# Two linear-attention and MLP layers on one core: half of layer one's sum of phi(K) moved from TensorE to GpSimd and VectorE, with a new written-out order

## The chip, the core and the metric

The kernel runs on one core of a Trainium2 chip. The core has five engines that run side by side and wait for one another by semaphores: TensorE (PE in the profile; its weight loads are PEld), VectorE (DVE), ScalarE (ACT), GpSimd (POOL) and SyncE (SP), which here only issues DMAs. Matmul results land in PSUM, eight banks of 128 x 512 fp32; everything else works in SBUF. The metric is the device time of one execution in microseconds (us), the median of the runs shown. Lower is better.

## What is computed

The reference takes x (2048 tokens of 512 features, bf16) through four residual steps: attention block, MLP block, and both again with the same weights.

```python
# attention block, on y = layernorm(x), 32 heads of 16
q, k, v = split(y @ wqkv)
phi = lambda t: where(t > 0, t + 1, exp(t)) + 1e-6
kv  = einsum("bhsd,bhse->bhde", phi(k), v)
z   = einsum("bhsd->bhd", phi(k))               # sum of phi(k) over all tokens
o   = einsum("bhqd,bhde->bhqe", phi(q), kv) / (einsum("bhqd,bhd->bhq", phi(q), z) + 1e-6)
x   = x + o @ wo
# MLP block
x   = x + gelu(layernorm(layernorm(x)) @ w1 + b1) @ w2 + b2
```

The change is about z in the first of the two layers: for each of the 512 features of K, the sum of phi(K) over 2048 tokens.

## The kernel before

**Tiles.** Tokens are cut into 16 tiles of 128 (numbered 0 to 15) and these into four chunks of four. A tile of x has 128 tokens on the partitions and 512 features in the free dimension. Chunk c of x is one slot of the buffer t4.

**Layer one, start.** For each tile: statistics on DVE (`statsA0_n`, L775, and `aggrA0_n`, L777; tile 3's on ACT), the variance plus epsilon (`veps`, L782, on POOL or DVE), its power -0.5 on POOL (`pow`, L784), sometimes the negated mean times that (`nmr`, L795, POOL), and the norm on DVE (L803) or ACT (L798). Tiles 0 to 3 are transposed by PE (L825) and copied out by ACT (L835), tiles 0 and 1 from a version that is only centred (L789). For Q, and for all other tiles, the transpose is a DMA that SP issues (`TA0_n`, L812). Then come `K0_n` (L879, four matmuls of 128x512), phi of it, and `G0_n` (L984), which adds y^T phi(K) up in four PSUM banks that stay taken through the first 45 us; so K and Q share the other four. Q of chunk 0 is L909 and has features on the partitions; Q of the other chunks is L896 and has tokens on the partitions.

**phi** (function `phi`) is exp on ACT (L847), relu on ACT (L858), min with 1 on DVE (L851 or L860, called `mink` or `minq`), and a sum on DVE or POOL (L864). For tiles marked "max" there is no relu: DVE reads the bank once more (L853). A bank is free for the next K or Q when the last of these that read it is done.

**The sum z** (function `attn_z`). For each chunk c of layer one, `Z0_c` is 16 matmuls (L970): a 128x128 block of phi(K) as the weights, one column of ones as the moving operand, four tiles added up for each of four feature blocks. `zs0_c` on DVE copies (c = 0, L944) or adds (L941) the 128x4 result into `zs`. In layer two it is done another way for chunks 0 to 2: `za1` to `za11` add the phi(K) tiles up in the fp32 tile `zacc` (L958, on POOL or DVE), `zhi` (L923) rounds the sum to bf16 in `dz`, `zlo` (L926) takes the rest in bf16, and `ZH` (L933, L934) runs eight one-column matmuls, two for each feature block, on the two halves.

**What needs z.** `zb0` on DVE (L1040) spreads zs over a mask; `D0_0_k` on PE (L1100) takes zb as its weights and gives the denominators of chunk 0, whose logarithm and exponential ACT takes (L1102, L1104). `dz0` on DVE (L1045) and `ZR0` on PE (L1048) give zs as a row, which ACT copies (`cpz0`, L997) and the other chunks' denominators use (`pz`, L1077; `pr`, L1089 or L1108).

**After that**: G is copied to gtb (L1000, `cpg`), multiplied with Wv (L1034), masked (L1053, `kvm`), multiplied with Wo (L1057), and for each tile come the attention's output (L1123), its residual add, the norms of the MLP, the MLP's first matmul (L1153) with gelu on ACT (L1158), and the second (L1190). The last tile's is split (L1176).

**The order** is written out: `CONF` holds one list of operation names for each engine (`ORDER`), the buffer slot of each tile (`PLACES`) and the engine that does an operation where there is a choice (`WAY`). `Settled` takes these as they stand, `assign_waits` sets the semaphore waits, and each engine runs its list from front to back. Every operation waits for its inputs and for the readers of whatever lay in its slot before. `LOADS` names the first DMAs in their order. The `za` adds are one chain, since each reads and writes zacc.

The lines of `attn_z` that choose between the two ways, in before and after alike:

```python
by_sum = [int(v) for v in (eng("zc0") or "").split()] if L == 0 else list(range(NC - 1))
...
if L == 0 and by_sum and c == max(v for v in range(NC) if v not in by_sum):
    fold(True)
```

`eng("zc0")` looks the name up in `WAY`. Without it `by_sum` is empty in layer one.

Of the kernel before, what the change touches and what calls it, by code (L numbers as in the profile page):

```python
# [185 lines left out]
def assign_waits(graph, order, sems, dma_sems):  # L186
# [10 lines left out]
    while len(done) < total:  # L197
        moved = False
        for e in ENGINES:
# [84 lines left out]
        "act":  # L284
# [1075 lines left out]
```

## Time and profile before

| what | us |
|---|---|
| median of 3 runs | 323.21 (323.02 to 324.14) |
| the profiled execution | 323.1 |
| its span, first to last instruction | 321.9 |
| PE busy | 318.0 |
| DVE / ACT / POOL busy | 218.1 / 189.3 / 145.5 |

How to read it: the span is the time from the first to the last instruction of the profiled execution, and the execution's own time has a little around it. Busy times are sums over the span; matmuls are pipelined, so a PE that is busy may still be held up between matmuls, and the chain of work that ended last tells where. The granted TensorE clock was 1.00 throughout. The prediction quotes whole lines of the page and of answers of the trace. A line of a group gives line of code, engine, operation, output<-inputs, count, and times. A timeline line gives start and length in us. Line numbers are those of the kernel before; in the kernel after they are one higher from `build_kernel` on.

### The profile page before, as it was taken

Reading aid. Unit: us, or ns where it says so; the run is one execution under the profiler, and the core shown is the slowest. Engines: PE = TensorE matmul, PEld = TensorE weight load, DVE = VectorE, ACT = ScalarE, POOL = GpSimd, SP = SyncE. Lnnn points to the kernel's source line nnn. Section 1 sums busy time; section 2 is a strip of 40 time slices with the busy share of each in tenths; the row PEclk is TensorE's granted clock in tenths of the full one; section 3 lists DMA queues with packets and bytes.
Section 4 is the critical chain, followed back from the end, with each engine's and each line's share of the span. In section 5 each row is a group of like instructions: output and inputs, shape, how many; then the busy total and the mean of one; then the engine's idle time right before and its main releaser. Section 6 shows DMA issues by size and latency. Waiting matters only on the chain.

```text
span 321.9 us, 4748 instructions
## 1 busy us (share of the span) xinstructions
PE 318.0 (99%) x1703; PEld 157.4 (49%) x1703; DVE 218.1 (68%) x529; ACT 189.3 (59%) x324; POOL 145.5 (45%) x216
## 2 busy tenths in 40 slices
PE   8999999999999999999999999999999999999997
PEld 3444554666444444444444444558544444444444
DVE  5998789999786774028848899999889881101103
ACT  5898656797730636667962367979634442663320
POOL 6573978688655355101822415887454163000000
DMA  7844793142121412111010200122232322201002
GB/s 257 200 81 85 241 348 85 35 82 36 33 49 34 82 33 51 34 33 32 18 40 10 51 16 0 35 51 52 50 62 54 98 65 67 49 0 35 16 33 65
DMA packets 52355, 21.68 MB, mean 67 GB/s; under 512 B 47532, under 2 KB 50860, under 8 KB 52332
## 3 DMA queue, kind: packets, MB, share of 16 engines
q1 hardware_dynamic: 50844, 16.37, 22.4%
q0 software_dynamic: 1056, 4.72, 4.3%
q10 hardware_dynamic: 432, 0.30, 0.3%
q8 instruction: 13, 0.21, 0.3%
q14 instruction: 10, 0.08, 0.1%
HBM read 8.00 MB, written 2.10 MB: 31 GB/s over the span
## 4 chain that ended last, share of the span: by engine, by line
PE 97%; DMA 2%; DVE 0%; issue 0%
PE ps L1153 30%; PE ps L1190 29%; PE ps L1123 9%; PE ps L879 8%; PE ps L896 6%; PE ps L984 4%; PE ps L1013 4%; DMA t<-in_A_x_dram 2%; PE ps L909 2%; PE ps L1176 1%; PE ps L970 1%; PE ps L1034 1%; PE ps L1057 1%; PE ps L1100 1%; DVE stats L775 0%; PE ps L1048 0%
## 5 line engine op out<-in xcount | busy, mean ns | idle before, releaser
L1158 ACT ACTIVATE gT<-ps,b1c 128x512 bf16<-128x512 f32 (+1 forms) x140 | 77.0, 601 | 68.7 <-PE ps L1153 68.1
L1153 PE MATMUL ps<-t,w 128*128 128x512 bf16 (+1 forms) x560 | 102.5, 336 | 0.0
L1190 PE MATMUL ps<-w,gT 128*128 128x512 bf16 x434 | 98.6, 379 | 0.0
L1153 PEld LDWEIGHTS ps<-t,w 128*128 128x128 bf16 x560 | 54.8, 98 | 43.7 <-ACT gT L1158 0.2
L1190 PEld LDWEIGHTS ps<-w,gT 128*128 128x128 bf16 x434 | 42.5, 98 | 50.4
L784 POOL TENSOR_TENSOR rstd<-veps,neghalf 128x1 f32<-128x1 f32 x64 | 39.0, 625 | 41.1 <-DVE veps L782 38.9
L847 ACT ACTIVATE eb<-ps 128x512 bf16<-128x512 f32 x62 | 35.4, 606 | 19.3 <-PE ps L896 7.3
L1200 DVE TENSOR_TENSOR yb<-ps,xsb 128x512 bf16<-128x512 f32 x15 | 10.2, 688 | 41.4 <-PE ps L1190 41.4
L775 DVE BATCH_NORM_STATS2 stats<-xsb 128x6 f32<-128x512 f32 x48 | 32.0, 681 | 0.3
L1123 PE MATMUL ps<-gtb,t 128*128 128x512 bf16 x128 | 31.4, 379 | 0.0
L879 PE MATMUL ps<-wqkv,t 128*128 128x512 bf16 x128 | 30.9, 379 | 0.3 <-ACT t L835 0.3
L858 ACT ACTIVATE rb<-ps 128x512 bf16<-128x512 f32 x43 | 25.3, 607 | 5.8 <-PE ps L879 5.8
L798 ACT ACTIVATE yb<-xsb,nmr,rstd 128x512 bf16<-128x512 f32 x21 | 16.9, 814 | 15.1 <-POOL nmr L795 15.1
L896 PE MATMUL ps<-wqkv,t 128*128 128x512 bf16 x96 | 24.1, 379 | 0.0
L1089 POOL TENSOR_TENSOR t<-t,rr 128x512 bf16<-128x512 bf16 x18 | 19.3, 1072 | 9.0 <-DVE rr L1085 6.4
L782 POOL TENSOR_SCALAR veps<-mv 128x1 f32<-128x1 f32 x35 | 8.2, 236 | 32.7 <-DVE mv L777 31.3
L1196 DVE TENSOR_TENSOR xsb<-ps,xsb 128x512 f32<-128x512 f32 x16 | 10.8, 678 | 17.9 <-PE ps L1190 17.9
L1139 POOL TENSOR_TENSOR xsb<-xsb,b2b 128x512 f32<-128x512 f32 x17 | 21.4, 1267 | 3.0 <-DVE yb L803 2.9
L1077 POOL TENSOR_TENSOR lr<-t,zrow 128x512 f32<-128x512 bf16 x14 | 16.5, 1179 | 7.3 <-ACT zrow L997 4.5
L1123 PEld LDWEIGHTS ps<-gtb,t 128*128 128x128 bf16 x128 | 12.5, 98 | 14.5
L803 DVE TENSOR_SCALAR yb<-xsb,mv,rstd 128x512 bf16<-128x512 f32 x27 | 14.5, 542 | 7.3 <-POOL rstd L784 6.0
L879 PEld LDWEIGHTS ps<-wqkv,t 128*128 128x128 bf16 x128 | 12.1, 98 | 14.7 <-ACT t L835 0.9
(99 smaller groups left out, 363.7 us busy)
## 6 DMA issues: line engine op xcount, KB each, us to landing
w<-in_B_w_dram POOLq DMA_DIRECT2D x4, 896.0 KB, 9.1
out_dram<-yb SPq DMA_DIRECT2D x15, 128.0 KB, 2.0
t<-in_A_x_dram SPq DMA_DIRECT2D x3, 512.0 KB, 4.8
t<-yb SPq DMA_TRANSPOSE x62, 2.5
wqkv<-in_A_wqkv_dram SPq DMA_DIRECT2D x1, 512.0 KB, 5.9
wqkv<-in_A_wqkv_dram POOLq DMA_DIRECT2D x1, 512.0 KB, 4.7
wo<-in_A_wo_dram POOLq DMA_DIRECT2D x1, 512.0 KB, 5.3
t<-in_A_x_dram SPq DMA_DIRECT2D x1, 384.0 KB, 3.3
```

The lines of the kernel that those rows point to most:

```text
L775: G.op("dve", lambda e: e.bn_stats(stats[:, s.slot, :], src()), 620, reads=src_keys, writes=[k + "s"], tiles=[s, *src_tiles], name=f"stats ...
L784: G.op("pool", lambda e: e.tensor_tensor(rstd[:, s.slot:s.slot + 1], veps[:, s.slot:s.slot + 1], neghalf[:], op=ALU.pow), 570, reads=[k + ...
L847: G.op("act", lambda e: e.activation(eb[:, et.slot, :], bank(bt), ACT.Exp, scale=by()), 478, reads=[src_key, *more_keys], writes=[f"e{tag} ...
L858: G.op("act", lambda e: e.activation(rb[:, rt.slot, :], bank(bt), ACT.Relu, scale=by()), 478, reads=[src_key, *more_keys], writes=[f"r{tag ...
L879: ins = e.matmul(bank(b), lhsT=yTa(yT)[:, dt, k * P:(k + 1) * P], rhs=wqkv[:, dt, D:2 * D], start=(i == 0 and n == 0), stop=(i == len(part ...
L896: ins = e.matmul(bank(b), lhsT=yTa(yT)[:, dt, k * P:(k + 1) * P], rhs=wqkv[:, dt, 0:D], start=(dt == 0), stop=(dt == DT - 1))
L1089: lambda e, d=d, tok=tok, heads=heads: e.tensor_tensor(heads(tok()), heads(tok()), rr[:, d.slot, :].unsqueeze(2).broadcast_to([P, H, DH]), ...
L1123: ins = e.matmul(bank(wb), lhsT=yTa(pq)[:, kt, k * P:(k + 1) * P], rhs=gtb[:, kt, :], start=(kt == 0), stop=(kt == DT - 1))
L1139: G.op("pool" if on_pool else "dve", lambda e: e.tensor_tensor(xsb[:, st, :], xsb[:, st, :], b2b[:], op=ALU.add), 1120 if on_pool else 600 ...
L1153: ins = e.matmul(bank(b, n), lhsT=w1[:, dt, ft * P:(ft + 1) * P], rhs=yTa(yT)[:, dt, k0 * P:k1 * P], start=(dt == 0), stop=(dt == DT - 1))
L1158: G.op("act", lambda e, ft=ft, b=b, k0=k0, k1=k1, n=n: e.activation(gT[:, g.slot, ft * 512 + k0 * P:ft * 512 + k1 * P], bank(b, n), ACT.Ge ...
L1190: ins = e.matmul(bank(b), lhsT=gT[:, g.slot, ft * 512 + k * P:ft * 512 + (k + 1) * P], rhs=w2[:, ft, :], start=(ft == 0), stop=(ft == FT - 1))
```

## The change

Only `CONF` changes; no line of the functions does. One entry is added, and it takes chunks 0 and 1 of layer one through the way that layer two has:

```diff
-        "za9": "pool",
+        "za8": "pool", "za9": "dve", "zaA2": "dve", "zc0": "0 1",
```

So `Z0_0`, `Z0_1`, `zs0_0` and `zs0_1` are gone. In their place stand `zaA1` to `zaA7`, which add the phi(K) of tiles 0 to 7 up in zacc (`zaA2` on DVE, the other six on POOL), `zhiA`, `zloA` on DVE, `ZHA` on PE with eight one-column matmuls, and `zshA` on DVE, which adds its result to zs. `Z0_2` and `Z0_3` stay.

`ORDER`, `PLACES` and `WAY` are written anew for the whole kernel. `LOADS` and the place of the x loads among SP's operations are as before: the third chunk's load, `xc2`, still stands behind `TA0_0` and `TA0_1`. 36 operations go from POOL to DVE and 24 from DVE to POOL (`pz`, `pr`, `b2`, `veps`, `za`), the rest stay on their engines. The lists around the change, cut to where the sums are made and used:

```diff
 "pe":
-  PTA0_3 K0_2 K0_3 G0_0_0 G0_1_0 Q0_0_2 Q0_0_1 Q0_0_0 K0_5 G0_2_0 K0_4 Z0_0 G0_3_0 Q0_1_0 K0_7 Q0_1_3 K0_6
-  G0_4_0 G0_5_0 Q0_1_2 K0_13 K0_14 G0_6_0 K0_12 Z0_1 K0_15 K0_10 K0_8 K0_9 K0_11 G0_7_0 Q0_1_1 Z0_3 Q0_0_3
-  Z0_2 G0_8_0 G0_9_0 D0_0_2 G0_10_0 D0_0_0 G0_11_0 ZR0
+  PTA0_3 K0_2 K0_3 G0_0_0 G0_1_0 Q0_0_0 Q0_0_1 Q0_0_2 Q0_1_0 K0_4 G0_2_0 G0_3_0 K0_5 K0_7 K0_6 G0_4_0 Q0_1_3
+  G0_5_0 K0_15 Q0_1_2 K0_12 K0_13 G0_6_0 K0_14 K0_10 K0_8 K0_11 K0_9 G0_7_0 Q0_0_3 Z0_3 G0_8_0 Z0_2 Q0_1_1
+  ZHA G0_9_0 D0_0_2 G0_10_0 ZR0 G0_11_0
 "dve":
-  normA0_0 vepsA0_1 normA0_2 statsA0_5 normA0_3 aggrA0_5 normA0_1 statsA0_4
+  normA0_2 normA0_0 normA0_1 statsA0_4 normA0_3
...
+  phik0_3 minq0_0_1 zaA2 aggrA0_12 mink0_4 statsA0_10 vepsA0_12 phik0_4 phiq0_0_1 aggrA0_10 statsA0_11
+  statsA0_8 aggrA0_11 normA0_12 mink0_5 aggrA0_8 phik0_5 minq0_1_0 minq0_0_0 phiq0_1_0
...
-  phik0_9 phik0_11 zs0_2 zs0_3 zb0
+  mink0_8 zhiA phik0_10 mink0_9 mink0_11 phik0_9 phik0_11 zloA zs0_2 minq0_0_3 zs0_3 zshA zb0 dz0
 "pool":
+  powA0_4 vepsA0_7 powA0_7 vepsA0_5 nmrA0_7 zaA1 powA0_5 vepsA0_6 vepsA0_13 powA0_13 powA0_6 nmrA0_13 vepsA0_15
+  powA0_15 vepsA0_14 nmrA0_15 powA0_14 nmrA0_14 zaA3 powA0_12 zaA4 vepsA0_10 powA0_10 nmrA0_10 vepsA0_11
+  vepsA0_8 zaA5 powA0_8 nmrA0_8 powA0_11 nmrA0_11 vepsA0_9 powA0_9 zaA6 zaA7 phik0_14 phik0_8 b1z wv wo
 "sp":
-  xc1 wq xc3 TA0_0 TA0_1 xc2 TA0_5 TA0_4 TA0_7 TA0_6 TA0_13 TA0_14
+  xc1 wq xc3 TA0_0 TA0_1 xc2 TA0_4 TA0_7 TA0_5 TA0_6 TA0_13 TA0_15
```

The other orders differ all through in the same manner, by neighbours that change places.

469 rows, old and new, of tables (ORDER, PLACES, WAY) are left out of this document.

## The prediction

> **What bounds the kernel now.** I read the busy shares of the page first, then the waits of PE, then the chain that ended last. All times are us of the profiled execution: span 321.9, its own time 323.1, so 1.2 lie around the span; the median of the runs shown is 323.21, 0.11 above it.
>
> The page's busy times, by engine:
>
> ```profile
> PE 318.0 (99%) x1703; PEld 157.4 (49%) x1703; DVE 218.1 (68%) x529; ACT 189.3 (59%) x324; POOL 145.5 (45%) x216
> ```
>
> PE is busy 99% of the span, the others far less. The page warns that a busy PE need not be at its peak, so the next view is who PE waited for, over the whole span:
>
> ```profile
> PE ps L749 <- PEq L1345: 0.8, 1, 0.8
> PE ps L825 <- DVE yb L803: 0.5, 1, 0.5
> PE ps L879 <- ACT t L835: 0.3, 1, 0.3
> PE ps L825 <- DVE yb L789: 0.2, 1, 0.2
> ```
>
> 1.8 us in four waits. The chain that ended last (start, length, what) tells where they end:
>
> ```profile
> 8.09 0.69 DVE stats L775
> 8.79 0.33 DVE yb L803
> 9.12 0.04 issue
> 9.16 0.40 PE ps L825 x4
> 9.56 1.73 PE ps L879 x8
> ...
> 18.19 0.38 PE ps L970 x16
> 18.57 0.89 PE ps L984 x4
> ```
>
> Until 9.16 the start waits for the load of x's second chunk (lands 8.07), the statistics queued behind it on DVE, and the fourth tile's norm. From 9.16 the chain is PE alone to 319.94, every 128x512 matmul 0.216 after the last (0.86 for four). So from 9.16 on the time is the sum of what PE is given, and a removed matmul shortens it by its spacing, provided no new wait appears. L970 is the sum of phi(K) that the change halves: 16 one-column matmuls take 0.38, and the group behind them 0.89 instead of 0.86, so 0.41 a call.
>
> **What it removes and adds on PE.** Removed: Z0_0 and Z0_1, 2 x 0.41 = 0.82. Added: ZHA, 8 matmuls of one column. Its like is layer two's ZH (L933/L934): first matmul 189.24, next group 189.44, so 0.20. Net on PE: 0.62 less. Everything else on PE is the same set in another order (1703 - 32 + 8 = 1679 matmuls).
>
> **The wait it adds.** The sums zs feed zb, zb feeds D0_0_2 (L1100). In before, these rows stand there (timeline):
>
> ```profile
> 37.08 0.36 DVE L941 TENSOR_TENSOR zs<-ps,zs 128x4 f32<-128x4 f32 x2 [0.77 <-PE ps L970]
> 37.48 0.69 DVE L1040 TENSOR_TENSOR zb<-bdmask,zs 128x512 bf16<-128x512 bf16 x1
> ...
> 38.63 0.38 PE L1100 MATMUL ps<-t,zb 128*128 128x512 bf16 x1
> ```
>
> zb ends at 38.17, D0_0_2 starts at 38.63: two groups G (2 x 0.86) cover it, with 0.46 to spare. In the new order only G0_9 stands between ZHA and D0_0_2. From ZHA's start: 0.34 to the end of its last matmul, 0.04 to DVE, 0.15 for zs, 0.04, 0.69 for zb, 0.06 to PE (as from yb at 9.10 to L825 at 9.16) = 1.32. PE has 0.20 + 0.86 = 1.06 to do. So 0.26 of idle PE is new. Behind D0_0_2 everything on PE waits too. If the chain is shorter than these rows it is nothing; a DVE instruction ahead of zs could add one length, 0.69, but DVE then stands before zs waiting for it.
>
> **The adds.** Layer two has the same instruction; the rows of the tile zacc give POOL 1156/1158/1337 ns (min/median/max) and DVE 658/688/694. Six on POOL are 6 x 1.16 = 7.0 us, one on DVE 0.69, then the two halves 0.42 and 0.68 (rows L923, L926) and zs 0.15, less two zs of 0.15: DVE +1.6. In the stretch from 12.1 to 29.2, where the adds must run, POOL is busy 10.3 of 17.1 us: with 7.0 more it is full, to about 29.3. What is queued behind them are the powers and means of later x tiles (L784, L795), which DVE's and ACT's norms wait for, then SP's transposes, then PE. I laid the new order out from 9.16 with the durations of these rows, PE in steps of 0.86:
> - zaA1 must wait for phi(K) of tile 1 (about 11.8), and runs to 13.3. The power of tile 5 is behind it (13.9 instead of 10.3), its norm on DVE about 14.8, its transpose goes out behind tile 7's at 14.9 and takes the 2.5 of the DMA rows: 17.4. K0_5 is the 12th group after 9.39, at 18.9: 1.5 to spare.
> - The first transposed tile now is tile 4's (norm 12.1, issued 12.15, landed about 14.7), needed at 15.4 by Q0_1_0: 0.7 to spare, where before tile 5 landed at 15.1 for a use at 15.4.
> - Later transposes go out 1.31 apart from 17.5, two or three us before their K.
> - zaA7 ends at 29.2; phik0_14 behind it has its inputs at about 30.4. The halves end near 35.4, ZHA is reached near 37.0. All hidden.
> - wv's load, issued by POOL behind phik0_8, leaves some 1 us later (33.5 instead of 32.5), lands at 38, and KV uses it at 45.
>
> So the adds cost nothing as long as DVE keeps these dates. DVE is 27.4 of 30.8 us busy from 9.16 to 40; 1.6 more makes 94%, so that cover is thin.
>
> **Start, loads, tail.** The list of loads is unchanged; the load of x's third chunk still stands behind TA0_0 and TA0_1 on SP. The norm of tile 1 moves ahead of the statistics that wait for chunk two, so TA0_1 leaves at about 8.8 instead of 9.52 and that load about 0.7 sooner: nobody waits for it. The norm of tile 3 still stands behind statistics of chunk two (now tile 4's), so 9.16 stays. The last PE groups and the output are in the same order. These count zero. pr0_0_0 moves from POOL to DVE ahead of the copies of G (L1000): the last copy that KV needs ends some 0.2 to 0.3 before its use; zero too.
>
> **Sum.** -0.82 + 0.20 + 0.26 = -0.36: 323.1 - 0.36 = 322.7 by the profiled execution, 322.85 by the median. I say **322.8**.
>
> **The rule against it.** When a DVE instruction meets a long POOL one, rows show it stretched (timeline at 153 and at 156):
>
> ```profile
> 153.05 1.68 POOL L1139 TENSOR_TENSOR xsb<-xsb,b2b 128x512 f32<-128x512 f32 x1
> 153.06 0.66 DVE L958 TENSOR_TENSOR zacc<-zacc,pkb 128x512 f32<-128x512 f32 x1
> ...
> 153.63 1.25 DVE L860 TENSOR_SCALAR eb<-eb 128x512 bf16<-128x512 bf16 x1
> ```
>
> ```profile
> 156.32 1.22 POOL L864 TENSOR_TENSOR pkb<-eb,rb 128x512 bf16<-128x512 bf16 x1 [0.24 <-DVE eb L860]
> 156.44 0.68 DVE L853 SCALAR_TENSOR_TENSOR pkb<-ps,eb 128x512 bf16<-128x512 f32 x1
> ...
> 157.05 0.78 DVE L864 TENSOR_TENSOR pkb<-eb,rb 128x512 bf16<-128x512 bf16 x1
> ```
>
> L860 takes 0.285 at the median and 1.25 here, ending when POOL ends; L864 on DVE 0.42 elsewhere, 0.78 here. Statistics (L775, 0.63 to 0.70 everywhere) and the form reading PSUM (L853) are not touched. The Trainium skill, "SBUF — State Buffer", section "Who interferes with whom", says why: GpSimd and VectorE share a pair of ports under an exclusive lock, taken by whichever starts first for its whole instruction, and a VectorE instruction with two SBUF inputs or in a two-port mode blocks against it. The trace agrees with 1.25 for 0.285. By the rows that I laid out the sum is 322.8; by that rule, with the adds ahead wherever an add and such a VectorE instruction come free together, it is the second rival's 323.8.
>
> **Rivals.**
> 1. The wait at D0_0_2 is hidden after all (ZHA arrives late behind another short wait, or zb is quicker): the full 0.62, 322.5. For it: 0.26 is a sum of small parts. Against: each part is a row. Chance 0.12.
> 2. **Slower: an add takes the ports ahead of a DVE instruction that frees a PSUM bank.** Two places meet: zaA3 and mink0_4, both free to start near 18.2 (both follow zaA2); zaA5 and minq0_0_0, both near 22.9 (both follow phik0_5). Price 1.25 - 0.285 = 0.96 each. Behind the first stands phik0_4 (ends near 20.0), whose bank K0_6 needs at 20.6: 0.96 - 0.6 = 0.36 of PE idle. Behind the second phiq0_1_0 (near 23.8), for K0_15 at 24.1: 0.96 - 0.3 = 0.66. Together 1.0: 322.8 + 1.0 = 323.8. It decides the sign once the two exceed 0.36. For it: DVE has little slack there and both engines are released by the same event. Against: in before, the short POOL powers met DVE instructions in this very stretch and L860 stayed at 0.29; POOL often lost instead (powers of 0.85 and 1.11 for 0.55). Chance 0.21.
> 3. The new order stalls PE behind 40 us: 36 instructions go from POOL to DVE and 24 back, and all orders change. Before, PE had no wait there, with margins down to 0.2 (a gelu to the matmul that takes its bank). Two or three places late by a DVE row of 0.69 give 1.4 to 2.1: 324.2 to 324.9. Against: total work of each engine hardly changes and DVE is 68% busy. Chance 0.11.
> 4. The change does not do what it says (the sums' matmuls were free): 323.1 + 0.26 = 323.4. The 0.41 per call is measured spacing on a packed PE, so 0.02.
>
> The forecast holds 0.54.
>
> **How the numbers follow.** Low end: the full 0.62 under the lowest run shown (323.02), 322.4. High end: into the third rival, 324.6; some of it, and what I have not seen, is left out. 0.5% is 1.6 us, about what a measurement of this kernel can tell from no change. Faster by that (below 321.6) would need more than PE loses: 0.02. Slower by that (above 324.8) is the far end of the third rival and two mishaps of the second at once: 0.08. The rest, 0.90, is within 0.5%.
>
> **What would show it.** L970 x48 instead of x80, and L933/L934 x8 twice; on the chain, one idle piece of 0.2 to 0.3 before the first L1100, released by zb. If PE's waits show L879 or L909 released by DVE pkb or t between 18 and 32, with DVE L860 or L851 above 0.5 us there, the second rival is at work. POOL's gap before phik0_14, 4.94 us now, should fall to about 1. I am wrong if the chain's packed part starts elsewhere than near 9.2, or if PE waits beyond 45 us.

## The result

The changed kernel takes **328.0 us** (median of 6 runs, 326.88 to 328.2); the kernel before, on the same chip, 323.06 (6 runs, 322.56 to 324.14). The ratio is 1.014, with a 95% interval of 1.012 to 1.016: **slower by about 1.4%**. The prediction said 322.8, no change, with a range up to 324.6. The profiled execution of the changed kernel took 328.1, its span is 326.5 (before: 321.9).

Lines in after.py stand one further down than in before.py, so L970 is now L971, L879 is L880 and so on. Busy times of the changed kernel, by engine:

```profile
PE 319.5 (98%) x1679; PEld 156.3 (48%) x1679; DVE 226.4 (69%) x543; ACT 189.8 (58%) x324; POOL 147.5 (45%) x210
```

PE has 24 matmuls fewer, as the change says, and is still what the time follows. Whom PE waited for in the changed kernel (us in total, times, longest):

```profile
PE ps L880 <- DMA t<-yb: 1.1, 1, 1.1
PE ps L750 <- PEq L1346: 0.8, 1, 0.8
PE ps L1124 <- DMA t<-t: 0.8, 1, 0.8
PE ps L880 <- DVE pkb L854: 0.7, 1, 0.7
PE ps L880 <- ACT eb L848: 0.6, 2, 0.4
PE ps L1154 <- DMA t<-yb: 0.3, 1, 0.3
PE ps L826 <- DVE yb L790: 0.2, 1, 0.2
```

Before, the same view had three waits of PE behind its first instruction's, 0.5, 0.3 and 0.2, all ahead of 9.2 us. Now K matmuls (L880) wait for DVE and ACT, and three matmuls wait for a transposing DMA (`t<-yb`, `t<-t`). A wait hides part of a loss, because PE's records overlap; so I went through PE's matmuls from 9 us on and noted each start that comes later than the spacing of a packed PE allows (0.216 behind a 512-column matmul). Before, there is no such place. The changed kernel has ten, 5.33 us in all:

| where | PE lost | what came last |
|---|---|---|
| 19.7 to 33.3, six K and Q calls | 2.43 | exp, relu or phi of the tile that held the bank |
| 40.6, D0_0_2 | 0.26 | zb0 |
| 56.5, WO0_7_0 | 0.95 | the transpose TP0_1_3 |
| 111.6, K1_0 | 1.23 | the transpose TA1_0 |
| 219.7, W11_0_12_0 | 0.47 | the transpose TB1_1 |

5.33, less 0.62 for the matmuls taken out, less 0.21 because PE's packed part begins at 8.95 and not 9.16 (x's second chunk landed at 7.86 and not 8.07), is 4.5; the span grew by 4.6. So the loss has three parts: the first 40 us, the wait for zb, and three late transposes.

### The profile page after: what moved, and what is told of

It reads as the page before. It is cut to its first block, busy times and chain, and to the rows that moved or that the text cites. A ratio compares the mean times of both kernels' runs of the same rounds, so it can differ in the third digit from the quotient of the medians.

```text
span 326.5 us, 4699 instructions
## 1 busy us (share of the span) xinstructions
PE 319.5 (98%) x1679; PEld 156.3 (48%) x1679; DVE 226.4 (69%) x543; ACT 189.8 (58%) x324; POOL 147.5 (45%) x210
## 4 chain that ended last, share of the span: by engine, by line
PE 79%; POOL 8%; DMA 5%; DVE 4%; ACT 2%; issue 1%; DVEq 0%
PE ps L1154 30%; PE ps L1191 28%; PE ps L1124 6%; PE ps L880 5%; PE ps L1014 4%; DMA t<-yb 2%; PE ps L985 2%; PE ps L897 2%; POOL rstd L785 2%; DMA t<-t 1%; PE ps L910 1%; POOL t L1090 1%; POOL t L1109 1%; POOL zacc L959 1%; POOL lr L1078 1%
## 5 line engine op out<-in xcount | busy, mean ns | idle before, releaser
L1154 PEld LDWEIGHTS ps<-t,w 128*128 128x128 bf16 x560 | 54.7, 98 | 44.0 <-DMA t<-yb 0.8
L880 PE MATMUL ps<-wqkv,t 128*128 128x512 bf16 x128 | 31.9, 380 | 2.7 <-DMA t<-yb 1.1
L897 PE MATMUL ps<-wqkv,t 128*128 128x512 bf16 x96 | 24.6, 379 | 0.1
L783 POOL TENSOR_SCALAR veps<-mv 128x1 f32<-128x1 f32 x29 | 9.2, 318 | 31.9 <-DVE mv L778 30.1
L880 PEld LDWEIGHTS ps<-wqkv,t 128*128 128x128 bf16 x128 | 11.7, 98 | 19.2 <-ACT eb L848 1.6
L804 DVE TENSOR_SCALAR yb<-xsb,mv,rstd 128x512 bf16<-128x512 f32 x27 | 14.9, 555 | 7.5 <-POOL rstd L785 7.3
L1140 DVE TENSOR_TENSOR xsb<-xsb,b2b 128x512 f32<-128x512 f32 x22 | 16.3, 758 | 3.5 <-ACT yb L799 3.5
```

The source lines that it names most:

```text
L880: ins = e.matmul(bank(b), lhsT=yTa(yT)[:, dt, k * P:(k + 1) * P], rhs=wqkv[:, dt, D:2 * D], start=(i == 0 and n == 0), stop=(i == len(part ...
L897: ins = e.matmul(bank(b), lhsT=yTa(yT)[:, dt, k * P:(k + 1) * P], rhs=wqkv[:, dt, 0:D], start=(dt == 0), stop=(dt == DT - 1))
L1154: ins = e.matmul(bank(b, n), lhsT=w1[:, dt, ft * P:(ft + 1) * P], rhs=yTa(yT)[:, dt, k0 * P:k1 * P], start=(dt == 0), stop=(dt == DT - 1))
```

## What the first 40 us show

This is the changed kernel's timeline at two of the places (start, length, engine, line, out<-in):

```profile
19.11 1.16 POOL L959 TENSOR_TENSOR zacc<-zacc,pkb 128x512 f32<-128x512 f32 x1
19.31 1.23 DVE L865 TENSOR_TENSOR t<-eb,rb 128x512 bf16<-128x512 bf16 x1
...
24.32 1.15 POOL L959 TENSOR_TENSOR zacc<-zacc,pkb 128x512 f32<-128x512 f32 x1
24.41 1.35 DVE L865 TENSOR_TENSOR t<-eb,rb 128x512 bf16<-128x512 bf16 x1
...
28.94 2.39 POOL L959 TENSOR_TENSOR zacc<-zacc,pkb 128x512 f32<-128x512 f32 x2
29.39 0.85 DVE L852 TENSOR_SCALAR eb<-eb 128x512 bf16<-128x512 bf16 x1 [0.38 <-ACT eb L848]
30.17 1.31 DVE L804 TENSOR_SCALAR yb<-t,mv,rstd 128x512 bf16<-128x512 bf16 x1
```

The adds are zaA3, zaA5, zaA6 and zaA7. Beside each stands a DVE instruction that elsewhere takes 0.42 (L865), 0.285 (L852) or 0.40 (L804), and that ends 0.15 to 0.3 behind the add. Added up against the medians of before, DVE's instructions between 9 and 40 are about 4 us too long; in before it is about half a us. Two of the lines between 9 and 38 us, first before, then changed (busy us, mean ns):

```profile
L803 DVE TENSOR_SCALAR yb<-t,mv,rstd 128x512 bf16<-128x512 bf16 x6 | 2.4, 398 | 0.0
L864 DVE TENSOR_TENSOR t<-eb,rb 128x512 bf16<-128x512 bf16 x4 | 1.6, 412 | 0.0
```

```profile
L865 DVE TENSOR_TENSOR t<-eb,rb 128x512 bf16<-128x512 bf16 x4 | 3.4, 852 | 0.0
...
L804 DVE TENSOR_SCALAR yb<-t,mv,rstd 128x512 bf16<-128x512 bf16 x5 | 2.9, 584 | 0.0
```

## The experiments

Theory A, after the comparison: an add on POOL costs DVE nearly its own length, by the ports (this part is called A1), DVE's time is what the first 40 us lack, and the late waits are the cost of transfers that moved. Theory C: the new orders lose by themselves. Theory A2: not the ports, but the powers queued on POOL behind the adds. The twelve runs were taken in three groups, each with its own runs of the kernel before (medians 323.07, 323.13, 323.02).

| kernel | median | ratio to before, 95% | PE lost 9 to 38 | at D0_0_2 | later |
|---|---|---|---|---|---|
| 1 orders only | 323.94 | 0.9989 to 1.005 | 0.94 | 0 | 0 |
| 2 sum only | 328.11 | 1.012 to 1.022 | 5.23 | 0.26 | 0.22 |
| 3 spare adds | 328.46 | 1.015 to 1.019 | 4.48 | 0 | 0.96 |
| 4 spare memsets | 325.42 | 1.005 to 1.012 | 2.44 | 0 | 0 |
| 5 adds on DVE | 324.38 | 1.002 to 1.007 | 1.68 | 0.26 | 0.84 |
| 6 late adds | 326.51 | 1.007 to 1.016 | 2.21 | 0.26 | 0.90 |
| 7 one chunk | 324.16 | 1.0015 to 1.005 | 0.84 | 0.26 | 0 |
| 8 24 warm-ups | 325.93 | 1.006 to 1.013 | 2.51 | 0.26 | 0.46 |
| 9 before, 104 warm-ups | 324.65 | 1.003 to 1.007 | 0 | 0 | 0.54 |
| 10 weights sooner | 328.07 | 1.012 to 1.019 | 3.37 | 0.26 | 1.34 |
| 11 denominator later | 327.73 (one run) | none | 2.60 | 0 | 1.21 |
| 12 orders, mended | 323.33 | 1.0001 to 1.0022 | 0.33 | 0 | 0 |

The last three columns are read from each kernel's one trace, as in the table above. In run 10 the loss at Z0_2, at 38.9, is counted with the front.

### Is it the adds or the orders?

**1. Orders only.** On the changed kernel:

```
-  "zc0": "0 1"                       +  "zc0": ""
-  pool: zaA1 zaA3..zaA7    dve: zaA2 zhiA zloA zshA    pe: ZHA
+  pe:  ... G0_2_0 Z0_0 G0_3_0 ...  K0_13 Z0_1 G0_6_0 ...
+  dve: ... phik0_4 zs0_0 ...       phiq0_1_2 zs0_1 ...
```

> The changed kernel's orders with the sums of the first two chunks back on PE (Z0_0 and Z0_1, zs0_0 and zs0_1; no adds). Theory A: the losses of 18 to 34 (2.43) come from the adds; without them POOL issues wv's and w1's loads some 4 us sooner (0.95 at WO0_7_0 goes) and PE's code loads stand against the work as in the kernel before (1.23 at K1_0 goes): 323.06 - 0.21 (the earlier start) = 322.9, with up to 0.5 for TB1_1. Rival C: the new orders lose by themselves: the three late stalls stay (2.65), 325.5; if the early ones stay too, 327.9.

Measured 323.94, with 0.94 us of PE lost: 0.43 at K0_5 and 0.34 at Z0_1, both from where I put Z0 and zs0, and 0.17 in the start. A had said 322.9 and is 1.0 short of it; C's least was 325.5. The 2.43 and all three late waits are gone. Theory C falls: the two places for Z0 and zs0 were new in this run, and with one of them mended (run 12, 323.33) the orders cost at most 0.3.

**2. Sum only.** On the kernel before, Z0_0, Z0_1, zs0_0 and zs0_1 out, and:

```
+  pool: powA0_4 zaA1 | nmrA0_14 zaA3 | powA0_12 zaA4 | powA0_10 zaA5 | nmrA0_11 zaA6 zaA7
+  dve:  phik0_3 zaA2 | mink0_8 zhiA | phik0_11 zloA | zshA zb0      pe: G0_8_0 ZHA
```

> The kernel before, its orders kept, with only the sums of the first two chunks moved to adds, put between the same neighbours as in the changed kernel where they exist (zaA1 after powA0_4, zaA2 on DVE after phik0_3, zaA3 after nmrA0_14, zaA4 after powA0_12, zaA5 after powA0_10, zaA6 and zaA7 after nmrA0_11), ZHA after G0_8. Theory A: PE gives back 0.62, and pays for DVE instructions stretched by the adds and powers queued behind them, 1.5 to 2.5 between 16 and 37, and 0.3 to 0.7 at D0_0_2; POOL issues the weights only 0 to 2 us later: 324.3 to 325.7. Rival C (the orders, not the adds): 322.4 to 322.9.

Measured 328.11: more than either theory gave. The direction is A's, the size is not: 2.33 at Q0_1_2 and 2.90 at K0_15 are lost, since here the stretched instructions stand just ahead of the two that PE needs. What an add costs depends on which DVE instruction it meets.

### Ports or queue?

**3. Spare adds.** The kernel before, nothing taken out, six adds on POOL that nobody reads:

```
+  G.op("pool", ... tensor_tensor(zacc, onesm if i == 1 else zacc, onesm, add) ..., name=f"ex{i}")   for i in 1, 3 to 7
+  pool: powA0_4 ex1 | nmrA0_14 ex3 | powA0_12 ex4 | powA0_10 ex5 | nmrA0_11 ex6 ex7
```

> The kernel before, PE, DVE, ACT and their orders untouched, with six extra adds of 128x512 on POOL that nobody reads (fp32 sum of a bf16 tile of ones), at the places where the second of the experiments had zaA1 and zaA3 to zaA7 (behind powA0_4, nmrA0_14, powA0_12, powA0_10, nmrA0_11). Theory A1, the ports: some five DVE instructions without a PSUM operand take 0.6 to 1.0 more (sum 3 to 4.5), and PE loses 2 to 5 between 16 and 37: 325 to 328. Theory A2, POOL's queue alone: DVE's instructions keep their lengths (sum below 1); the loss is what the late powers cost.

Measured 328.46, PE loses 4.48 between 9 and 38, and DVE's instructions are 5.1 us too long. This is the whole front loss, and more, with neither a matmul removed nor an order changed. Time and stretch lie a little above what A1 gave (325 to 328, 3 to 4.5). **4. Spare memsets.** The same, with `memset(gacc[:, 0:2, :], 0.0)` in place of each add:

> The same as the spare adds, with each of the six replaced by a POOL memset of 128x1024 fp32 that nobody reads, 0.9 to 1.2 us by the 128x128 memset's 0.2 in the trace of before: about the same time in POOL's queue, and no SBUF operand read. Theory A2, the queue: the same loss as the spare adds. Theory A1, the ports, as far as it hangs on the add's two reads: DVE's instructions keep their lengths and the loss is below 1 (323.1 to 324). If a write alone holds the ports too, DVE is stretched as by the adds and the two cannot be told apart here.

A memset took 0.95, and the loss is 2.44, with DVE's instructions 3.4 us too long: the branch in which a write alone holds DVE up, and by the expectation's words the time of this run cannot then tell ports from queue. The loss falls by more than the queue alone would have it: a memset is 82% of an add (1.16) in POOL's queue, the loss 54% of the 4.48. What tells the two apart is which instructions are stretched, and not every DVE instruction is. First the spare adds' timeline, then the spare memsets':

```profile
19.59 1.16 POOL L698 TENSOR_TENSOR zacc<-zacc,onesm 128x512 f32<-128x512 f32 x1
19.65 1.25 DVE L851 TENSOR_SCALAR eb<-eb 128x512 bf16<-128x512 bf16 x1 [0.45 <-ACT eb L847]
```

```profile
18.73 0.95 POOL L698 MEMSET gacc<- 128x1024 f32 x1
18.82 1.01 DVE L851 TENSOR_SCALAR eb<-eb 128x512 bf16<-128x512 bf16 x1 [0.45 <-ACT eb L847]
...
28.14 1.99 POOL L698 MEMSET gacc<- 128x1024 f32 x2
29.16 0.41 DVE L864 TENSOR_TENSOR t<-eb,rb 128x512 bf16<-128x512 bf16 x1
29.49 0.78 DVE L851 TENSOR_SCALAR eb<-eb 128x512 bf16<-128x512 bf16 x1
```

mink0_4 (L851, 0.285 alone) takes the length of whatever POOL runs beside it: 1.25 beside an add, 1.01 beside a memset. phiq0_0_0 (L864), which has two SBUF inputs, keeps its 0.41 beside a memset; beside an add it took 1.38 in the run with spare adds. phik0_1, the same form, does so too, at 11: 0.43 beside the first memset, 1.14 beside the first spare add. A queue on POOL would delay DVE's instructions; here they are lengthened while they run. The Trainium skill, "SBUF — State Buffer", section "Who interferes with whom", says just this: a VectorE instruction with two SBUF inputs contends with a GpSimd instruction that reads SBUF, not with one that only writes, while VectorE in a two-port mode contends with GpSimd, and whoever issues first holds the shared pair for its whole instruction. The trace does not show in which mode mink0_4 ran; its length fits the second of these. The statistics and the form that reads PSUM kept their lengths in all traces, which agrees as well.

**5. Adds on DVE.** From here to the one-chunk run the base is the changed kernel with 24 extra warm-ups (run 8, 325.93, told below), so that the late waits stay out of the way.

```
-  pool: zaA1 zaA3 zaA4 zaA5 zaA6 zaA7
+  dve: minq0_0_1 zaA1 zaA2 | phiq0_0_1 zaA3 | phiq0_1_0 zaA4 | phiq0_0_0 zaA5 | phiq0_1_2 zaA6 | phiq0_1_3 zaA7
```

> The changed kernel with the 24 extra warm-ups and all seven adds on DVE, each where its input is there (zaA1 and zaA2 behind minq0_0_1, the others each behind a phi(Q)): POOL does none, so neither its queue nor the ports hold them up, and DVE has 6 x 0.69 = 4.1 us more to do, where the adds on POOL stretched its other instructions by 3.4 us more than before. Theory A1 (DVE's time is what is short, whether the adds take it themselves or by the ports): the loss between 10 and 36 stays 2 to 3.5, 325.5 to 327. Theory A2 (POOL's queue): the powers are on time and the loss falls to 1 or less, 324.4 or less.

**6. Late adds.** On POOL, `zaA3 zaA4 zaA5` from their places to `powA0_9 zaA3 zaA4 zaA5 zaA6 zaA7 phik0_14`:

> The changed kernel with the 24 extra warm-ups, and on POOL zaA3, zaA4 and zaA5 moved behind powA0_9, ahead of zaA6: no power or mean of an x tile is queued behind them any more. The 24 extra warm-ups alone gave 325.9, with 2.5 us of PE lost between 10 and 34. Theory A1, the ports: DVE instructions stretched by the adds are what PE waits for; all five adds now lie in 26 to 33, beside the phi(K) work that frees PSUM banks just in time, so the loss moves there and stays 1.5 to 2.5: 325 to 326. Theory A2, POOL's queue: the powers and means behind the adds are what came late; the loss falls below 0.7: 323.7 to 324.2.

With all adds on DVE: 324.38, a front loss of 1.68, and DVE's stretch is down to 0.4. With late adds: 326.51, 0.5 above A1's range, as much as WO0_7_0 lost again (0.49); a front loss of 2.21, a stretch of about 4. In run 8 and with the adds on DVE, 0.3 of the front loss is something else: the transposes TA0_6 (4.82) and TA0_5 (4.28) have a 16 KB code load inside (the section on late transposes tells of these), and K0_6 and K0_5 wait for them. Without that, run 8 has 2.21, late adds 2.21, adds on DVE 1.39. So taking the powers out from behind the adds gains nothing, and the loss moves to K0_14 to K0_9, as A1 said. For the adds on DVE neither band fits: the median lies at A2's edge, the front loss in between.

That does not make POOL's queue free. The chain that ended last (start, length, what), first of the changed kernel, then with late adds:

```profile
19.15 1.11 POOL zacc L959
...
20.93 1.15 POOL zacc L959
...
24.32 1.15 POOL zacc L959
25.47 0.80 POOL rstd L785
...
29.39 0.85 DVE eb L852
30.25 1.23 DVE yb L804
```

```profile
26.87 1.18 DVE eb L852
...
29.26 1.23 DVE yb L804
...
31.86 1.16 DVE eb L852
```

In the changed kernel it runs through POOL from 14.0 to 28.1, with zaA3, zaA4 and zaA5 on it and the powers between them; only then through the stretched instructions of DVE. With late adds it leaves POOL out from 18 to 35, and goes through stretched DVE instructions; with the adds on DVE it goes through DVE, adds included, from 17.8 to 31.2. So in the changed kernel both limits lay close together. Lifting the queue alone left the loss as it was, so DVE's time is enough for it; that the queue alone would have been enough is not shown. The busy times between 9 and 38 us show how full DVE is (us of the stretch, then PE, PEld, DVE, ACT, POOL, each with its number of instructions; then clock, DMA share, GB/s); in order the kernel before, orders only, changed, and adds on DVE:

```profile
9.00:38.00 29.00, 28.84 (x194) 13.88 (x195) 25.68 (x78) 25.33 (x46) 18.16 (x39) 1.00 0.57 126
```

```profile
9.00:38.00 29.00, 28.55 (x192) 13.33 (x190) 24.13 (x74) 23.99 (x44) 16.98 (x37) 1.00 0.46 92
```

```profile
9.00:38.00 29.00, 27.50 (x141) 11.59 (x142) 28.20 (x73) 24.19 (x44) 22.67 (x39) 1.00 0.44 93
```

```profile
9.00:38.00 29.00, 28.26 (x155) 12.08 (x159) 28.72 (x82) 24.40 (x44) 18.56 (x36) 1.00 0.54 90
```

Behind PE, DVE is the busiest engine: 24.1 us of 29 with the sums on PE, 28.2 with six adds on POOL and one on DVE, 28.7 with all seven on DVE, which had got further by 38 us (82 DVE instructions for 73, six of them the adds). So I counted the same instructions in each trace, all that DVE does from the statistics of x's second chunk to ahead of zs0_2, and added what the sums take on DVE up to there (two at once counted once): 25.1 us with the sums on PE, 29.8 with six adds on POOL, 29.6 with all on DVE. **Six adds, 4.1 us of DVE's time, moved to POOL and freed nothing on DVE.** That is the main finding. The DVE version is quicker, as I read it, because its DVE time falls where the list puts it; from POOL it falls on whatever DVE is doing. This is not shown: late adds, whose powers stand behind no add either, still lose 2.21, but their adds also lie later. Its trace is of an execution of 326.4, 2.0 above the median: 0.84 of that is a slow transpose (TB0_1, 4.13), 1.2 a longer stretch from the last matmul to the last output's landing (3.1 for 1.9).

**7. One chunk.** `"zc0": "0"`, zaA4 to zaA7 out, Z0_1 ahead of G0_6_0 and zs0_1 behind phiq0_1_2, 16 extra warm-ups:

> The changed kernel with only the first chunk added up (zaA1 and zaA3 on POOL, zaA2 on DVE); the second chunk's sum is back on PE as Z0_1, ahead of G0_6_0 with its zs0_1 behind phiq0_1_2; 16 extra warm-ups in place of 24, so that PE's code loads stay where they are in the kernel before. Theory A1 and A2 alike: what zaA4 to zaA7 cost goes (most of 2.5), zaA3 still stretches phiq0_0_1 (0.1 to 0.5 at K0_7 and K0_6), Z0_1 costs up to 0.34 for its place and 0.41 for itself against ZHA's 0.20, D0_0_2 0.26: 323.2 to 324.2. If the cost does not grow with the adds but comes from the fold (zhiA, zloA, ZHA) and the orders: 325.5 and more.

Measured 324.16, inside the range. The front loss falls to 0.84, and none of it stands behind an add: 0.32 at K0_6 is TA0_6 again (4.84, with a 16 KB code load inside), 0.24 is at Z0_1, 0.17 in the start, 0.11 at K0_7 behind a relu. zaA3 did stretch phiq0_0_1 to 1.23, but here PE lost nothing by it. So the fold and the orders cost no more than this, and with two POOL adds in place of six the loss by stretched instructions is gone; how it grows in between one such run does not say.

### The late transposes

**8. 24 warm-ups.** PE starts with 15 matmuls that compute nothing (`WARM`, L750). On the changed kernel:

```
-  WARM=[[512, 512, 512, 512, 512, 512, 512], [256] x8]
+  WARM=[[512, 512, 512, 512, 512, 512, 512], [64, 64, 64, 64] x8]
```

> The changed kernel with 24 more warm-up matmuls on PE ahead of the first real one (each of the eight 256-column warm-ups cut into four of 64 columns); nothing else. In the trace of the changed kernel TA1_0's transpose took 4.54 us instead of 2.4 and K1_0 lost 1.23 us of PE to it; a 16 KB transfer on the queue of kind instruction lies inside it (at 108.2). Theory A, code loads: these transfers come every 110 to 150 matmuls of PE, so the 24 matmuls taken out move them against the work; 24 warm-ups put them back near the place of the kernel before (W20_6_0), TA1_0 is quick again, K1_0 waits for nothing: 328.0 - 1.2 = 326.8. Rival B, order: TA1_0 is slow because TP0_3_1 now goes out just ahead of it; then the 1.23 stays: 328.0. The stalls of PE between 18 and 34 should stay at 2 to 2.6 by both.

Measured 325.93: 2.1 less for cutting up warm-ups. SP's DMAs in the changed kernel, TP0_3_1, TA1_0 and TP0_3_3, with K1_0's matmuls:

```profile
104.72 1.27 SPq L1094 DMA_TRANSPOSE t<-t  x1
106.97 1.19 SPq L813 DMA_TRANSPOSE t<-yb  x1
108.72 2.26 SPq L1094 DMA_TRANSPOSE t<-t  x1
...
111.56 0.60 PE L880 MATMUL ps<-wqkv,t 128*128 128x512 bf16 x2 [1.07 <-DMA t<-yb]
```

and with 24 warm-ups:

```profile
103.79 1.27 SPq L1094 DMA_TRANSPOSE t<-t  x1
106.05 1.19 SPq L813 DMA_TRANSPOSE t<-yb  x1
107.79 1.19 SPq L1094 DMA_TRANSPOSE t<-t  x1
...
109.41 0.81 PE L880 MATMUL ps<-wqkv,t 128*128 128x512 bf16 x3
```

The order is the same, TP0_3_1 ahead of TA1_0 in both, so rival B falls: TA1_0 now lands in 2.4, and K1_0 loses nothing. The DMA queues of the changed kernel between 107 and 110 us (packets, MB, share of 16 engines):

```profile
q1 hardware_dynamic: 507, 0.12, 76.6%
q8 instruction: 1, 0.02, 3.5%
```

The second line is one packet of 16 KB, at 108.23, for 1.69 us; with 24 warm-ups the nearest such packet comes at 101.3. I take these for loads of program code: the queue's kind is instruction, and in the trace of before one comes every 110 to 149 matmuls of PE. 24 matmuls fewer put them at other places of the work, and one of the new places is TA1_0. The 0.95 at WO0_7_0 went too, which I had not said: TP0_1_3 took 3.64 for 4.79, w2_1 landed at 54.7 for 55.9. The loads were issued at the same times; a 16 KB load at 44.4 lies among them in the changed kernel and comes at 39.2 here, which is not tried alone. The 0.46 at W11_0_12_0 stayed: an 8 KB code load on another queue (q14), which the warm-ups of PE don't move against the work, lies in TB1_1.

**9. Before, with 104 warm-ups.** The kernel before, and only:

```
+  WARM=[[32] x62 + [64] x25, [64, 64, 64, 64] x8]
```

> The kernel before with its 15 warm-up matmuls cut into 119 of the same columns in all (62 of 32, 57 of 64): 104 more, nothing else. One 16 KB transfer of the queue of kind instruction holds about 128 matmuls of PE, so 104 more ahead should put these transfers where 24 fewer would, as in the changed kernel: one at about 104.7, 0.6 behind the issue of TA1_0 (104.08). Theory A, code loads: TA1_0 takes about 4.1 to 4.5 instead of 2.4, lands at 108.2 to 108.6, and K1_0 (107.43) waits 0.8 to 1.2, with up to 0.6 more from other transposes: 323.9 to 324.9. Rival B: the place of the code loads does not matter, 323.0 to 323.3.

Measured 324.65, within the range, but not by the wait that I named. A code load did come at 105.2 and TA1_0 took 3.02, yet K1_0 did not wait. PE lost 0.54 at WO1_8_0 instead, whose transpose TP1_2_0 (3.73 for 2.42) has one inside, and 0.62 in the start: a code load at 5.4 stands among the first loads, x's second chunk lands at 8.69 instead of 8.07, and PTA0_3 starts at 9.78 instead of 9.16. So an unchanged computation gets 0.5% slower with 104 more warm-ups, as I read it because PE's code loads move; where each one hits was not to be foreseen from the count.

Over the traces of all 14 kernels, of the transposes issued after 60 us, the 808 that have no code load beginning between 0.2 before and 2.2 after their issue take 2.45 at the median, and 3 of them over 3. The 53 with a 16 KB load take 3.41 at the median and up to 4.54 (37 over 3), the 69 with one of 8 KB 2.62 (26 over 3).

**10. Weights sooner.** On the changed kernel's POOL list, `zaA7 phik0_14 wv wo phik0_8 b1z w1_0` for `zaA7 phik0_14 phik0_8 b1z wv wo w1_0`:

> The changed kernel with wv's and wo's loads issued on POOL right behind phik0_14, ahead of phik0_8 and b1z, as in the kernel before; nothing else. Theory A: WO0_7_0 lost 0.95 because TP0_1_3's transpose ran beside the weight loads (w2_1 landed at 55.9, the transpose took 4.79 instead of 2.43); wv leaves some 3 us sooner, w2_1 lands near 52 to 53, the transpose is quicker and the 0.95 goes or shrinks to 0.3: 327.1 to 327.4. Rival B: the transpose is slow for another reason: 328.0.

w2_1 lands at 52.1, TP0_1_3 takes 2.42, the 0.95 is gone: A was right on the cause. But 328.07: issuing two loads held phik0_8 up, and 0.82 was lost at G0_8 and Z0_2. K1_0 still lost 0.87.

**11. Denominator later.** On the 24 warm-ups, `ZHA G0_9_0 G0_10_0 D0_0_2` for `ZHA G0_9_0 D0_0_2 G0_10_0`:

> The changed kernel with the 24 extra warm-ups and, on PE, D0_0_2 behind G0_10_0 instead of ahead of it; nothing else. If the 0.26 at D0_0_2 is zb that comes late, one G group (0.86) covers it and PE waits for nothing there; the rest as with the warm-ups alone: 325.9 - 0.26 = 325.7. If it is something of D0_0_2 itself, the gap goes along with it.

The 0.26 is gone, as it should if zb is late. The time, 327.73 in its one run, says nothing on 0.26: in this execution x's second load landed at 5.73 instead of 4.6 and PE's packed part began at 9.92 instead of 8.89, and 0.62 was lost at two waits near M0 and WO0_0 that the run with 24 warm-ups alone doesn't have. Whether D0_0_2's move made those two I did not try.

**12. Orders, mended.** As in run 1, `mink0_4 zs0_0 statsA0_10` for `phik0_4 zs0_0 phiq0_0_1`:

> The changed kernel's orders with both sums back on PE (as in the order-only run), and zs0_0 moved on DVE from behind phik0_4 to behind mink0_4. There K0_5 waited 0.43 for zs0_0 (19.39 to 19.54, its matmuls done at 18.44). Expected: zs0_0 ends near 18.65, K0_5 waits for nothing; the 0.34 at Z0_1 stays: 323.94 - 0.4 = 323.5, with the kernel before's 323.1 as the mark that the orders alone do not pass. If the wait moves to phik0_4 or phiq0_0_1 instead: 323.9.

323.33, with the 0.43 gone; still 0.1% above the kernel before. No version here beats the kernel before.

## Why the prediction was wrong

**What held.** PE lost 32 matmuls and gained 8; ZHA took its 0.20; the new wait at D0_0_2 was 0.26 to the hundredth, released by zb, and run 11 shows one more group covers it. TA0_4 was in time for Q0_1_0, with 0.21 to spare. The start's 0.21 is the landing of x's second chunk, which lies between 7.5 and 8.7 in the 14 traces.

**The step that failed**: "So the adds cost nothing as long as DVE keeps these dates." DVE could not keep them. I gave DVE 1.6 us more and called 94% a thin cover; it got 4.7 more than with the sums on PE (29.8 for 25.1, 3.4 of it in instructions that were stretched), was busy for 28.20 of 29.00, and freed banks late: 2.43. POOL did not keep the dates either: zaA7 ended at 31.3 and not 29.2, its gap before phik0_14 fell to 2.0 and not 1, and the chain shows its queue as close behind. ZHA came at 39.2 and not 37.0. The sign of being wrong that the prediction named, waits of PE beyond 45 us, came three times.

**The second rival had the mechanism**, at the wrong price and places. It gave the ports 1.0 us at mink0_4 and minq0_0_0; the trace shows phiq0_0_1, phiq0_0_0, mink0_12 and normA0_9, 3.2 us of DVE in all. I had the 1.25 of L860 in hand and set it against short POOL powers that lost to DVE, but a power of 0.55 says little of an add of 1.16. The right estimate was not where two instructions are released together, but how often an add of 1.16 finds DVE, 89% busy by my own count, at an instruction that needs the ports: four of six adds did in the changed kernel, all six in run 3, at 0.5 to 1.0 each.

**Two zeros that were not.** "wv's load ... uses it at 45" was worked out for wv alone, and put its issue at 33.5: it left at 38.1, as phik0_8 ran later and 1.28 more passed ahead of the issue in which POOL waited for nothing that the profile shows. The last of the weight loads behind it landed at 55.9 instead of 50.0, beside TP0_1_3: 0.95. And "everything else on PE is the same set in another order" left out the loading of PE's program, as I take it: 1.23, shown by run 8, and 0.47 beside the q14 load, which no run tries alone. The third rival had the place (behind 40 us), at 1.4 to 2.1 for the 2.65 measured, but not the cause: it blamed late DVE rows of the new orders, and in run 1 these orders lose nothing behind 38 us.

**Open.** How much of the 2.43 POOL's queue would have cost by itself, and why the adds on DVE lose less for the same DVE time. Why POOL waited 1.28 ahead of wv (an 8 KB code load at 36.3 lies next to it, not tried), which engine the q14 loads belong to and whether they make the 0.47 at W11_0_12_0, and why WO0_7_0 is relieved by 24 warm-ups.

## What to carry to other kernels

Before work goes to GpSimd to spare VectorE, read how busy VectorE is in that stage and which of its instructions need the shared ports: here the long GpSimd adds took from VectorE all that they would have cost there, so the move freed nothing. A few cheap matmuls on a packed engine can cost less than adds on an idle engine that take their time from the next busiest one. When a change of a fraction of a per cent alters the number of matmuls, look in the DMA queues for packets of kind instruction, which I take for code loads, and at the transposes they hit before blaming the change itself.

## What was not expected of the hardware

- What I take for loads of program code shows as packets of 16 and 8 KB on queues of kind instruction, and a transposing DMA that has one of 16 KB inside took 3.41 at the median, up to 4.54, for 2.45 without. Cutting warm-ups, which changes no work, moved the time by 2.1 us down in one kernel (328.0 to 325.9) and 1.6 up in another (323.0 to 324.65).
- A POOL memset of 0.95 stretched `tensor_scalar` on DVE (0.285 to 1.01) but left `tensor_tensor` at 0.41; an add stretched both (to 1.25 and 1.38).
- POOL loses too: vepsA0_14, 0.19 for a 128x1 result elsewhere, took 1.01 beside DVE's own add zaA2.
